# An attention layer with an MLP on one core: one PSUM tile per bank of the running sums, clamp on VectorE, the last batch's mixing moved behind the first pair of output tiles, a second buffer for staged sums

## The chip, the cores and the metric

The kernel runs as one program on one core of a Trainium2 chip. The metric is the device time of an execution in microseconds (us). Three runs of the kernel before took 904.13, 904.23 and 909.96 us; the median is 904.23 us.

## The reference

q, k and v have shape (4, 8, 576, 64): batch, heads, sequence, head width. The MLP works on rows of 512 (all heads side by side), 4 x 576 = 2304 rows, with 2048 hidden columns.

```python
scores = scale * np.matmul(q, k.transpose(0, 1, 3, 2))
x = (np.log1p(np.abs(rel)) / np.log1p(np.maximum(pos[:, None], 1.0)))[..., None]
bias = np.maximum(x @ w1 + b1, 0.0) @ w2
scores = scores + bias.transpose(2, 0, 1)[None]
attn = softmax(scores)                       # over the last axis
x = matmul(attn, v), heads side by side      # (B, S, 512)
u = x + (x.transpose(0, 2, 1) @ U @ V).transpose(0, 2, 1)
out = u + np.maximum(u @ w_ch1, 0.0) @ w_ch2
```

U, V, w_ch1 and w_ch2 arrive as 64-bit floats and are turned into 32-bit floats in the kernel.

## The kernel before

**Attention.** Batch and pair of heads give 16 pairs; each has nine slots of scores, softmax, transposes and products with v. The mixing with U and V (mix_t, mix_h) follows for each batch, and its rows go to u_dram. The code is written out by hand under a manual schedule: the order of the calls is the order on each engine's queue.

**MLP.** The 2304 rows are two sets of 1152 (st = 0, 1), the hidden columns eight blocks of 256 (F). That gives 16 stages n = 8 st + F, counted 0 to 15. In a stage the rows come in two units: u0 with 512 rows (matmuls 256 columns wide) and u1 with 640 rows (320 wide). mlp1 forms a unit's hidden values with seven block products in place of eight. Its four steps are a, b, c and d. Two products are summed on in one PSUM bank after earlier ones (first=False), so a bank is copied out between them:

```python
def a():   # tile p: sums A in bank 0, C in bank 1; tile q: B
    prod(1, k["a"]);  nc.scalar.copy(out=k["r1"], in_=k["a"])
    prod(5, k["c"]);  nc.scalar.copy(out=k["r5"], in_=k["c"])
def b():
    prod(6, k["a"], False);  nc.scalar.copy(out=k["r2"], in_=k["a"])
    prod(3, k["c"], False);  r2 = C + r2      # VectorE, L722
def c():
    prod(7, k["a"], False);  nc.scalar.copy(out=k["r3"], in_=k["a"])
    prod(2, k["b"]);  r3 = r3 + r5;  r1 = B + r1   # L728, L729
def d():
    prod(4, k["a"], False)   # then relu (ScalarE, L735) and the low part (VectorE, L736)
```

Every 32-bit operand is a high and a low part, so a product is six matmuls (L698), named ph in the trace. mlp2 multiplies one tile of 128 hidden rows of the stage before with w_ch2, six matmuls (L761, named po), and VectorE adds the result to acc (L763). A stage runs a, y, b, y, c, y, d, y for u0 with four tiles y, then the same for u1 with five.

**Preparing weights.** Beside the matmuls of stages 1 to 7 the weights of the next stage are converted from 64-bit words (conv): ScalarE size (L1122, L1123), GpSimd clamp (L1126), VectorE shift and join (L1132, L1136), GpSimd add (L1141), and a store to wy_dram. w1_prep then forms four sums (GpSimd, L648 to L651) and splits all seven blocks into high (ScalarE, L667) and low (GpSimd, L671); w2_prep does it for w_ch2 (L679, L682). These calls stand in a list, and background(n) takes groups from its front after each step, spread over the whole stage. Stages 8 to 15 load the converted words again.

**Rows of u.** build_u loads two tiles of u rows, transposes them on TensorE (L587, named tu), copies them (L593, L603), forms four sums (L609 to L612) and splits them (L623, L627). The first set's rows are built late in attention and in stage 0, the second set's in stages 7 and 8.

**Tiles and waits.** PSUM comes from pools: psS has two buffers of two banks, psT one and psT2 two of one bank (used in turn for tag t), psA one. An instruction waits for the engines that last used the same tile. p holds A and C in one tile.

Of the kernel before, what the change touches and what calls it, by code (L numbers as in the profile page):

```python
# [20 lines left out]
DM = H * D  # L21
# [29 lines left out]
PROD = {1: (0, 0), 2: (1, 1), 3: (6, 2), 4: (2, 6), 5: (3, 3), 6: (4, 4), 7: (5, 5)}  # L51
# [5 lines left out]
def kernel(  # L57
# [33 lines left out]
    p1, p2 = ExitStack(), ExitStack()  # L91

    def left(ctx, name, bufs, **kw):
        return ctx.enter_context(tc.tile_pool(name=name, bufs=bufs, side="left", **kw))
# [6 lines left out]
    mix = left(p1, "mix", 1)  # L101
# [26 lines left out]
    ptp = left(p1, "ptp", 1)  # L128
# [278 lines left out]
    def get_pt(p, hf):  # L407
        d = pair[p]
        if ("pt", hf) not in d:
            n, a = (320, LINE) if hf == 0 else (256, 0)  # L410
            t = ptp.tile([P, a + 9 * n], F32, tag=f"pt{hf}", name="pt")[:, a:]
            d["pt", hf] = t.rearrange("p (k q) -> p k q", k=9)
        return d["pt", hf]
# [220 lines left out]
    def w1_op(F, o, low):  # L634
        w = w1q[F]
        return w["b"][o][low] if o < 3 else w["t"][low][:, o - 3]

    def w1_prep(F, ys, t):

        y0, y1 = (y.rearrange("p (k f) -> p k f", k=2) for y in ys)  # L640
        b11, b12 = y0[:, :, 0:P], y0[:, :, P:]
        b21, b22 = y1[:, :, 0:P], y1[:, :, P:]
        tv = ops_view(t)
        both = y1.rearrange("p k (o f) -> p o k f", o=2)

        def sums():
            g = nc.gpsimd
            g.tensor_tensor(out=tv[:, 0], in0=b12, in1=b11, op=ALU.subtract)  # L648
            g.tensor_tensor(out=tv[:, 1], in0=b22, in1=tv[:, 0], op=ALU.subtract)
            g.tensor_tensor(out=tv[:, 2], in0=b22, in1=b12, op=ALU.subtract)  # L650
            g.tensor_tensor(out=tv[:, 3], in0=b21, in1=tv[:, 1], op=ALU.subtract)  # L651

        def trips(which):
            w = w1q[F]
            if "b" in which:
                yield *w["b"][0], b11
                if "two" in w:
                    yield *w["two"], both
                else:
                    yield *w["b"][1], b21  # L660
                    yield *w["b"][2], b22
            if "t" in which:
                yield *w["t"], tv

        def high(which):
            for h, _, x in trips(which):
                nc.scalar.copy(out=h, in_=x)  # L667

        def low(which):
            for h, l, x in trips(which):  # L670
                nc.gpsimd.tensor_tensor(out=l, in0=x, in1=h.bitcast(F32), op=ALU.subtract)  # L671

        return sums, high, low
# [12 lines left out]
    def mlp1(st, F, u, hid, rp):  # L686
# [183 lines left out]
    def open_tail():  # L870
# [5 lines left out]
        tl_p["b22"] = tp.tile([P, LINE + 4 * P], F32R, tag="b", name="w1b")[:, LINE:]  # L876
# [27 lines left out]
    def at_slot(p, s):  # L904
# [8 lines left out]
        elif (p, s) == (NP - 3, 1):  # L913
# [3 lines left out]
            }  # L917
        elif (p, s) == (NP - 3, 8):
# [12 lines left out]
        elif (p, s) == (NP - 2, 6):  # L931
            t = rawp.tile([P, QKW], F32R, tag="raw", name="w1t")
            w1q[0] = {
                "b": [hi_lo(x) for x in (*tl_p["spare"], tl_p["b22"])],
                "t": (ops_view(t[:, 0 : 8 * P]), ops_view(t[:, 8 * P : 16 * P])),
            }
# [7 lines left out]
        elif (p, s) == (NP - 1, 0):  # L944
            tl_p["prep"][1]("bt")
        elif (p, s) == (NP - 1, 1):
            tl_p["prep"][2]("bt")
            tl_p["u1h"] = big_u(2, 1)[0]
        elif p == NP - 1 and 4 <= s <= 8:
            b[0, 1][s - 3]()  # L950
            if s == 6:
                acc_tile(0)
            if s == 8:
                b[1, 0][0]()
# [18 lines left out]
    feed = iter(())  # L973
# [28 lines left out]
    def run(*steps):  # L1002
        for o in steps:
            o()

    hid_t = {}

    def hid(g, u):
        def get():
# [5 lines left out]
            t = hid_t["p"].tile([P, 4 * UNITS[1]], F32R, tag="h", name="hh")  # L1015
            return t[:, 0 : 2 * UNITS[1]], t[:, 2 * UNITS[1] :]
# [10 lines left out]
    run(m[0][0])  # L1027
    slot(NP, 1)
    acc_tile(2)
    run(b[1, 0][1], b[1, 0][2], m[0][1], b[1, 0][3], m[0][2], b[1, 1][0], b[1, 0][4])  # L1030
    slot(NP, 2)
    acc_tile(4)
    run(m[0][3], b[1, 0][5], b[1, 1][1], b[1, 1][2])
    run(y[0], b[1, 1][3], b[1, 2][0])
# [43 lines left out]
    def sum_tile():  # L1078
        return sump.tile([P, 1024], F32, tag="s", name="s")

    def w1_ready(g):
# [3 lines left out]
        def sums():  # L1085
            w1_tile(g)
            k["p"] = w1_prep(g, k["y"], sum_tile())
            k["p"][0]()

        def high():  # L1090
            k["p"][1]("bt")

        def low():
            k["p"][2]("bt")

        return k["y"], [sums, high, low]
# [9 lines left out]
    def conv(src, ys, dst):  # L1106
# [18 lines left out]
        def clamp():  # L1125
            nc.gpsimd.tensor_scalar(  # L1126
# [39 lines left out]
    def conv_groups(n):  # L1166
# [14 lines left out]
        queue.extend(groups)  # L1181

    def w1_y(F, i):
        if F < 2:
            return wq_dram[2 * i : 2 * i + 2, :, F * 2 * P : (F + 1) * 2 * P].rearrange("k p f -> p k f")
        return wy_dram[4 * F + i].rearrange("p (k f) -> p k f", k=2)

    def w2_y(F, j):
        return wq_dram[4 + 2 * F + j] if F < 2 else wy_dram[4 * F + 2 + j]
# [15 lines left out]
    def second_u():  # L1205

        def rows():
# [137 lines left out]
```

## Time and profile before

| | us |
|---|---|
| median of three runs | 904.23 |
| the profiled execution | 905.67 |
| its span, first to last instruction | 903.9 |
| PE busy / DVE / ACT / POOL | 766.7 / 511.3 / 445.6 / 419.7 |

The span is what the trace covers; 1.8 us of the profiled execution lie around it. PE is TensorE's matmuls, DVE VectorE, ACT ScalarE, POOL GpSimd. A matmul's busy time runs into that of the next one, since they are pipelined; so the time of a group is read from start to start. A row by stretch gives its bounds and length, the busy time of PE, PEld (weight load), DVE, ACT and POOL with the number of instructions, the granted clock, the DMA share and GB/s. A wait's three numbers are the total, how often, and the longest. In a timeline the bracket at the end of a row gives how long the engine sat idle before it, and who ended that.

### The profile page before, as it was taken

The numbers are of one execution on the slowest core, as the hardware profiler recorded it, in microseconds if no ns is written. First come the engines' busy times: TensorE is split into PE (matmuls) and PEld (weight loads), VectorE is DVE, ScalarE is ACT, GpSimd is POOL, SyncE is SP. The second block draws the span as 40 slices with busy tenths as digits, with TensorE's granted clock in tenths as the row PEclk, the third lists the DMA queues.
The fourth block names the chain that finished last, engine by engine and source line by source line (L and its number), as shares of the span: only waits on it lengthen the run. The fifth ranks groups of instructions, "written<-read, shape, count | busy, mean of one in ns | idle before, by whom it ended". The sixth has DMA issues, their size and how long they took to land. (4 is left out here: it accounts for less than half of the span.)

```text
span 903.9 us, 13221 instructions
## 1 busy us (share of the span) xinstructions
PE 766.7 (85%) x4748; PEld 609.0 (67%) x4748; DVE 511.3 (57%) x1085; ACT 445.6 (49%) x982; POOL 419.7 (46%) x321
## 2 busy tenths in 40 slices
PE   6788999999999978868877877878546999989998
PEld 3346777877776766657766766766435878878876
DVE  7965778777687665533655455444433344434434
ACT  7976677776767667423433433424322323233320
POOL 0025457655664473226777677656521433244310
PEclk9999999999999999996999899899677999999999
DMA  6989954556545531252222332332233311011002
GB/s 192 300 288 270 257 134 131 140 142 167 153 106 133 155 101 48 82 181 70 70 84 91 106 91 83 106 94 63 74 109 111 111 36 44 26 48 48 24 1 106
DMA packets 49218, 103.37 MB, mean 114 GB/s; under 512 B 7808, under 2 KB 12416, under 8 KB 47104
## 3 DMA queue, kind: packets, MB, share of 16 engines
q1 hardware_dynamic: 48912, 102.26, 38.4%
q8 instruction: 38, 0.62, 0.3%
q10 hardware_dynamic: 240, 0.26, 0.1%
q14 instruction: 28, 0.23, 0.1%
HBM read 73.78 MB, written 28.72 MB: 113 GB/s over the span
## 5 line engine op out<-in xcount | busy, mean ns | idle before, releaser
L698 PE MATMUL ph<-u,w 128*128 128x256 f32 (+1 forms) x1260 | 216.6, 313 | 73.1 <-ACT r L714 36.6
L698 PEld LDWEIGHTS ph<-u,w 128*128 128x128 f32 x1260 | 192.1, 200 | 103.5 <-ACT r L714 44.0
L763 DVE TENSOR_TENSOR acc<-po,acc 128x512 f32<-128x512 f32 x144 | 98.8, 689 | 156.1 <-PE po L761 154.4
L761 PE MATMUL po<-u,hh 128*128 128x512 f32 x648 | 180.1, 407 | 3.3 <-DVE acc L763 3.0
L761 PEld LDWEIGHTS po<-u,hh 128*128 128x128 f32 x648 | 118.8, 195 | 24.7 <-DVE acc L763 4.3
L376 ACT ACTIVATE p<-p,st 128x576 f32<-128x576 f32 x128 | 99.9, 781 | 43.9 <-DVE st L357 43.9
L357 DVE CUSTOM_DVE_ANT_0 p<-sc,bias 128x576 f32<-128x576 f32 x128 | 96.0, 750 | 39.9 <-PE sc L355 31.3
L355 PE MATMUL sc<-hi 128*128 128x288 f32 x320 | 101.4, 333 | 2.8 <-DVE st L357 2.7
L355 PE MATMUL sc<-lo,hi 128*128 128x288 f32 x320 | 90.1, 297 | 5.0 <-POOL lo L178 5.0
L461 PE MATMUL o<-pt,v 128*64 128x320 f32 (+1 forms) x640 | 91.2, 412 | 2.7 <-ACT pt L403 2.7
L172 POOL TENSOR_SCALAR hi<-raw 128x1216 fp32r<-128x1216 f32 x30 | 36.4, 1212 | 101.6 <-DMA raw<-in_qk_dram 85.1
L425 PE MATMUL tb<-ident,p 128*128 128x128 f32 x512 | 77.5, 274 | 2.8 <-DVE x_sb L405 2.3
L355 PEld LDWEIGHTS sc<-hi 128*128 128x128 f32 x320 | 60.7, 190 | 20.1 <-issue 10.7
L461 PEld LDWEIGHTS o<-pt,v 128*64 128x64 f32 x640 | 45.1, 136 | 37.9 <-ACT pt L403 7.3
L403 ACT COPY pt<-tb 128x512 f32<-128x512 f32 x88 | 50.9, 579 | 29.1 <-PE tb L425 28.2
L355 PEld LDWEIGHTS sc<-lo,hi 128*128 128x128 f32 x320 | 60.9, 190 | 6.5 <-POOL lo L178 5.9
L425 PEld LDWEIGHTS tb<-ident,p 128*128 128x128 f32 x512 | 61.8, 141 | 5.0 <-ACT p L376 4.1
L761 PE MATMUL po<-w,hh 128*128 128x512 f32 x216 | 64.2, 407 | 0.0
L671 POOL TENSOR_TENSOR w<-y,w 128x256 fp32r<-128x256 f32 (+1 forms) x30 | 29.8, 1015 | 61.4 <-ACT w L667 61.4
L1141 POOL TENSOR_TENSOR y<-wt,y 128x512 int32<-128x512 int32 x24 | 37.5, 1564 | 44.5 <-ACT wt L1122 14.1
L1126 POOL TENSOR_SCALAR wt<-wt 128x512 f32<-128x512 f32 x24 | 45.9, 1914 | 21.5 <-ACT wt L1122 21.5
L627 POOL TENSOR_TENSOR u<-sb,u 128x1024 fp32r<-128x1024 f32 (+1 forms) x10 | 22.4, 2244 | 63.9 <-ACT u L623 52.7
(129 smaller groups left out, 1241.5 us busy)
## 6 DMA issues: line engine op xcount, KB each, us to landing
raw<-in_qk_dram SPq DMA_DIRECT2D x31, 608.0 KB, 7.3
wraw<-in_w_ch_dram SPq DMA_DIRECT2D x24, 512.0 KB, 3.9
bias_dram<-ring SPq DMA_DIRECT2D x26, 295.5 KB, 4.2
wy_dram<-y SPq DMA_DIRECT2D x24, 256.0 KB, 2.2
y<-wy_dram SPq DMA_DIRECT2D x24, 256.0 KB, 2.6
v<-in_vp_dram SPq DMA_DIRECT2D x16, 320.0 KB, 8.2
bias<-bias_dram SPq DMA_DIRECT2D x16, 288.0 KB, 4.7
acc<-u_dram SPq DMA_DIRECT2D x18, 256.0 KB, 3.0
```

The lines of the kernel that those rows point to most:

```text
L172: nc.gpsimd.tensor_scalar(out=hi[:, a:e], in0=raw[:, a:e], scalar1=1.0, scalar2=0.0, op0=ALU.mult, op1=ALU.add)
L355: mm(ps[:, a, 0:HALF], lhsT=hi[:, q0 : q0 + P], rhs=kk, start=(i == 0), stop=(i == n - 1))
L357: nc.vector.tensor_tensor_reduce(out=halves(dst), in0=ps[:, :, 0:HALF], in1=halves(bias[hp][:, s * S : (s + 1) * S]), scale=-0.125, scalar ...
L376: nc.scalar.activation(out=dst, in_=dst, func=AF.Exp, bias=st[:, s : s + 1], scale=-1.0, accum_out=st[:, 10 + s : 11 + s])
L403: nc.scalar.copy(out=out, in_=in_)
L425: nc.tensor.transpose(bank[:, kb, :], src[:, b0 + kb * P : b0 + (kb + 1) * P], ident)
L461: mm(o[hd * D : (hd + 1) * D, 0:n], lhsT=v[:, vb * D : (vb + 1) * D], rhs=pt[:, pb, :], start=(j == 0), stop=(j == 4),)
L698: mm(out, lhsT=w1_op(g, w, a)[:, kt], rhs=b[:, o, kt, :], start=(first and c == 0), stop=(c == 5), skip_group_check=not first,)
L761: mm(ps, lhsT=lhs(x, f), rhs=w, start=(c == 0), stop=(c == 5))
L763: nc.vector.tensor_tensor(out=acc[i], in0=ps, in1=acc[i], op=ALU.add)
L1126: nc.gpsimd.tensor_scalar(out=k["t"].bitcast(F32), in0=k["t"].bitcast(F32), scalar1=F64_LO, scalar2=F64_HI, op0=ALU.max, op1=ALU.min,)
L1141: nc.gpsimd.tensor_tensor(out=k["y"], in0=k["t"], in1=k["y"], op=ALU.add)
```

## The change

It gives A and C a tile of psS each, and B a one-bank tile of tag t when its product comes. The clamp of conv goes to VectorE. w1_prep writes one of its sums over its input and splits the seven blocks in three groups of 512, 512 and 768 columns, each with its own steps. The rows of stage 0 are built earlier, with a staging buffer of their own for one of them (st); the weights of stage 1 are prepared in stage 0 in memory of their own. mix_t of the last batch stands behind the fourth output tile, and mix_h in stage 1. The work beside the matmuls is set by a plan, which spreads a list of groups over given steps. In stages 7 and 8 the rows of u use the buffers of conv.

```diff
         def a():
-            k["p"], k["q"] = psum("s", [P, 2, 512], "ph"), psum("s", [P, 2, 512], "ph")
-            k["a"], k["c"], k["b"] = k["p"][:, 0, 0:n], k["p"][:, 1, 0:n], k["q"][:, 0, 0:n]
+            k["a"], k["c"] = (psum("s", [P, 2, 512], "ph")[:, 0, 0:n] for _ in range(2))
...
         def c():
             prod(7, k["a"], False)
             nc.scalar.copy(out=k["r3"], in_=k["a"])
+            k["b"] = psum("t", [P, 512], "ph")[:, 0:n]
             prod(2, k["b"])
...
         def clamp():
-            nc.gpsimd.tensor_scalar(
+            nc.vector.tensor_scalar(
                 out=k["t"].bitcast(F32), in0=k["t"].bitcast(F32),
                 scalar1=F64_LO, scalar2=F64_HI, op0=ALU.max, op1=ALU.min,
             )
...
-                    then = ((1, 4, 5) if i else (), (1, 2))[g == n]
+                    then = ((1, 1, 2, 4, 5, 5, 6) if i else (), (2, 3))[g == n]
...
+            b[1, 1] = build_u(0, 1, 1, tl_p["row"], lambda k: tl_p["st"][:, (k == "sb") * 1024 :])
...
-    run(m[0][0])
+    run(b[1, 0][4], m[0][0], b[1, 0][5])
...
+    ts = [pmp.tile([P, S], F32, tag="praw", name="wt")[:, 0 : 4 * P], tl_p["row"]()[:, 0 : 2 * P]]
+    prep = w1_prep(1, ys, ts, True)
+    run(y[0], b[1, 2][4], b[1, 2][5], prep[0])
     slot(NP, 4)
-    run(b[1, 1][4], y[1], b[1, 1][5])
+    run(y[1], m[1][0])
     slot(NP, 8)
-    run(y[2], b[1, 2][1])
+    prep[1](1)
+    run(y[2], m[1][1])
...
     mix_t(B - 1)
-    run(b[1, 2][3], b[1, 2][4], b[1, 2][5], y[3])
-    mix_h(B - 1, 4)
-    run(m[1][0])
...
-    o = again(1, 0)
-    run(o[0], o[1], late_y[0], o[2], o[3], late_y[1], late_y[2])
...
         if n == 1:
-            first, second = [], late_y[3:]
+            h = [lambda c=c: mix_h(B - 1, c) for c in (4, 0, 1, 2, 3)]
+            y0, y1 = y1[0:3], y1[3:]
+            steps = []
+            for i in range(4):
+                steps += m[0][i : i + 1] + y0[i : i + 1] + h[i : i + 1]
...
+        def spread(groups, a, e):
+            for i, g in enumerate(groups):
+                plan[a + i * (e - a) // len(groups)] += g
...
+        else:
+            spread(work, 0, last - 1)
```

TensorE, start of a unit u1 in a late stage (ph_7758 is the tile that holds A and C, w1 the weights, u1_4028 and u1_4206 high and low weights kept beside the rows). Before:

```order
L698 MATMUL ph_7758<-u1_4028,w1_7519 128x320 [waits DVE_49]
L698 MATMUL ph_7758<-u1_4206,w1_7519 128x320
L698 MATMUL ph_7758<-u1_4028,w1_7519 128x320 x2
L698 MATMUL ph_7758<-u1_4206,w1_7519 128x320
L698 MATMUL ph_7758<-u1_4028,w1_7519 128x320
L698 MATMUL ph_7758<-u1_4028,w1_7519 128x320 [waits Activation_49]
```

The sixth row is the first matmul of product 5; it waits for ScalarE's copy of product 1 out of the same tile. The same place now (ph_7777 holds A, ph_7778 C):

```order
L699 MATMUL ph_7777<-u1_4026,w1_7504 128x320 [waits DVE_49]
L699 MATMUL ph_7777<-u1_4226,w1_7504 128x320
L699 MATMUL ph_7777<-u1_4026,w1_7504 128x320 x2
L699 MATMUL ph_7777<-u1_4226,w1_7504 128x320
L699 MATMUL ph_7777<-u1_4026,w1_7504 128x320
L699 MATMUL ph_7778<-u1_4026,w1_7504 128x320 [waits DVE_49]
```

Product 5 has the tile that held A in the unit before, and waits for VectorE's last read of it there (L737, L736 in the kernel before).

ScalarE, from the end of one stage into the next, among stages 3 to 6 (w is the high part of w_ch2; r and hh are mlp1's). Before:

```order
L726 COPY r<-ph 128x320 [waits DVE_49,PE_49]
L735 ACTIVATE hh<-r 128x960 [waits DVE_49]
L735 ACTIVATE hh<-ph 128x320 [waits PE_49]
L679 CAST w_4541<-y 128x512 [waits Pool_49]
L714 COPY r<-ph 128x256 [waits PE_49,Activation_49]
```

The cast waits for GpSimd's add of the last conversion, and the copy of product 1 stands behind it. In the changed kernel a cast that waits for GpSimd stands there too, and one more in the middle of the stage, between u0's relu and u1's copy:

```order
L736 ACTIVATE hh<-r 128x768 [waits DVE_49]
L736 ACTIVATE hh<-ph 128x256 [waits PE_49]
L666 CAST w_5118<-y 128x512 [waits Pool_49]
L1145 ACTIVATE wt<-wraw 128x512 [waits DMAHW6_49]
L1146 ACTIVATE y<-wraw 128x512 [waits DMAHW1_49,Activation_49]
L714 COPY r<-ph 128x320 [waits PE_49,Activation_49]
```

The casts of the split blocks have come forward, from behind u1's copies to ahead of them.

VectorE, a conversion at the turn from u0 to u1 of such a stage (wt and wraw are conv's). Before:

```order
L1132 TENSOR_SCALAR wt<-wt 128x512 [waits Pool_49]
L1136 SCALAR_TENSOR_TENSOR wt<-wraw,sgn,wt 128x512 [waits DMAHW4_49,DVE_49]
L736 SCALAR_TENSOR_TENSOR hh<-r,hh 128x768 [waits Activation_49]
L736 SCALAR_TENSOR_TENSOR hh<-ph,hh 128x256 [waits Activation_49]
L763 TENSOR_TENSOR acc<-po,acc 128x512 [waits PE_49] x2
```

And now:

```order
L1149 TENSOR_SCALAR wt<-wt 128x512 [waits Pool_49]
L764 TENSOR_TENSOR acc<-po,acc 128x512 [waits PE_49]
L1155 TENSOR_SCALAR wt<-wt 128x512 [waits DVE_49]
L1159 SCALAR_TENSOR_TENSOR wt<-wraw,sgn,wt 128x512 [waits DMAHW4_49,DVE_49]
L737 SCALAR_TENSOR_TENSOR hh<-r,hh 128x768 [waits Activation_49]
```

The clamp (L1149) has joined the queue a step ahead of the shift, and an acc addition stands between them.

## Rows read from the trace of the kernel before

**Rows 1.** The page: TensorE's granted clock, in 40 slices of the span.

```profile
PEclk9999999999999999996999899899677999999999
```

**Rows 2.** Busy time by stretch: stage 0, 1, 2, 3-6, 7, 8, 9-15.

```profile
357.29:402.43 45.14, 35.82 (x206) 26.48 (x204) 22.23 (x44) 17.83 (x35) 9.38 (x5) 1.00 0.31 101
402.43:431.63 29.20, 21.41 (x97) 18.34 (x97) 8.84 (x14) 11.29 (x22) 21.02 (x19) 0.71 0.30 102
431.63:460.47 28.84, 25.35 (x138) 21.17 (x139) 16.02 (x23) 13.74 (x26) 22.09 (x17) 1.00 0.26 82
460.47:595.90 135.43, 107.28 (x553) 90.77 (x552) 70.00 (x108) 52.39 (x100) 95.78 (x69) 0.92 0.28 94
595.90:640.29 44.39, 29.19 (x156) 23.80 (x154) 22.55 (x34) 16.05 (x29) 22.43 (x17) 0.91 0.29 89
640.29:699.40 59.11, 37.98 (x160) 31.25 (x161) 19.62 (x38) 16.96 (x29) 18.40 (x14) 0.75 0.26 86
699.40:887.00 187.60, 172.91 (x968) 149.83 (x967) 81.17 (x134) 59.36 (x117) 65.30 (x56) 1.00 0.14 42
```

**Rows 3.** Waits of TensorE, whole span: total us, times, longest.

```profile
PE ph L698 <- ACT r L714: 38.8, 32, 5.3
PE tu L587 <- DMA y<-u_dram: 17.6, 6, 5.7
PE ph L698 <- ACT r L720: 16.7, 32, 1.5
```

**Rows 4.** The chain that ended last, in stage 15: start, us, what.

```profile
860.25 0.72 PE ph L698 x6
861.47 0.97 PE ph L698 x6
...
872.29 0.89 PE ph L698 x6
873.74 1.15 PE ph L698 x6
...
884.23 15.33 PE po L761 x66
```

**Rows 5.** Timeline, from stage 3 into stage 4.

```profile
492.67 1.91 POOL L1126 TENSOR_SCALAR wt<-wt 128x512 f32<-128x512 f32 x1
...
495.96 2.05 POOL L1141 TENSOR_TENSOR y<-wt,y 128x512 int32<-128x512 int32 x1 [1.39 <-issue]
...
498.04 0.62 ACT L679 CAST w<-y 128x512 fp32r<-128x512 f32 x1 [4.75 <-POOL y L1141]
...
498.99 1.65 PE L698 MATMUL ph<-u,w 128*128 128x256 f32 x6 [5.31 <-ACT r L714]
```

**Rows 6.** Timeline: a GpSimd split and a VectorE sum at one time.

```profile
488.79 2.39 POOL L671 TENSOR_TENSOR w<-s,w 128x1024 fp32r<-128x1024 f32 x1
...
488.99 2.53 DVE L728 TENSOR_TENSOR r<-r,r 128x320 f32<-128x320 f32 x1 [2.54 <-ACT r L726]
```

**Rows 7.** VectorE's shift in the first conversions (a line's own view, 60 to 240).

```profile
L216 DVE TENSOR_SCALAR wt<-wt x15: 229/295/2876, 105.7 to 237.4; 128x256 int32<-128x256 int32 x13, 128x160 int32<-128x160 int32 x1, 128x128 int32<-128x128 int32 x1
```

**Rows 8.** TensorE's timeline ahead of stage 1.

```profile
402.43 0.50 PE L698 MATMUL ph<-u,w 128*128 128x256 f32 x2 [3.42 <-ACT w L667]
405.90 1.22 PE L698 MATMUL ph<-u,w 128*128 128x256 f32 x4 [2.97 <-POOL w L671]
```

**Rows 9.** TensorE's timeline: a flip in stage 7, and one in stage 8.

```profile
629.58 0.66 PE L587 MATMUL tu<-ident,y 128*128 128x128 f32 x4
629.99 1.65 PE L761 MATMUL po<-u,hh 128*128 128x512 f32 x6
...
671.95 1.09 PE L587 MATMUL tu<-ident,y 128*128 128x128 f32 x4 [5.71 <-DMA y<-u_dram]
```

**Rows 10.** Groups by line: the clamp, and VectorE's shift of the same width.

```profile
L1126 POOL TENSOR_SCALAR wt<-wt 128x512 f32<-128x512 f32 x24 | 45.9, 1914 | 21.5 <-ACT wt L1122 21.5
...
L1132 DVE TENSOR_SCALAR wt<-wt 128x512 int32<-128x512 int32 x24 | 10.1, 423 | 24.7 <-POOL wt L1126 24.7
```

More of the change, by code (lines that the diff above doesn't have):

```diff
@@ L100 @@
     vpp = left(ctx, "vpp", 2)
-    mix = left(p1, "mix", 1)
+    ptp = left(ctx, "ptp", 1)
+    mix = left(p3, "mix", 1, "right")
     bias_dram = dram.tile([S * H + 8, PITCH], F32, name="bias_dram")
@@ L634, in w1_op @@
     def w1_op(F, o, low):
[L635 to L644, printed above, removed]
+        g, i = ((0, 0), (0, 1), (1, 0), (1, 1), (2, 0), (2, 1), (2, 2))[o]
+        return w1q[F][g][low][:, i]
@@ L651, in sums @@
[L651 to L666, printed above, removed]
-                nc.scalar.copy(out=h, in_=x)
@@ L673, in w1_prep, with high, low @@
+        def high(g):
+            for h, _, x in trips(g):
+                nc.scalar.copy(out=h, in_=x)
+        def low(g):
+            for h, l, x in trips(g):
+                (nc.vector if fast and g < 2 else nc.gpsimd).tensor_tensor(
+                    out=l, in0=x, in1=h.bitcast(F32), op=ALU.subtract
+                )
         return sums, high, low
@@ L971, in pool, with w1_y, w2_y, run @@
         return left(ctx, name, bufs, reuse_waits="tile")
-    feed = iter(())
+    def w1_y(F, i):
+        if F < 2:
+            return wq_dram[2 * i : 2 * i + 2, :, F * 2 * P : (F + 1) * 2 * P].rearrange("k p f -> p k f")
+        return wy_dram[4 * F + i].rearrange("p (k f) -> p k f", k=2)
+    def w2_y(F, j):
+        return wq_dram[4 + 2 * F + j] if F < 2 else wy_dram[4 * F + 2 + j]
+    def run(*steps):
+        for o in steps:
+            o()
     for p in range(NP):
@@ L1085, in sums, with group, rest @@
         def sums():
-            w1_tile(g)
-            k["p"] = w1_prep(g, k["y"], sum_tile())
-            k["p"][0]()
[L1090 to L1096, printed above, removed]
+            if g % 2:
+                w1q[g] = w1q[1]
+            else:
+                t = hid_t["w1"].tile([P, W1 + LINE], F32R, tag="w1", name="w1")
+                w1q[g] = [hi_lo(t[:, a * P : e * P]) for a, e in ((0, 8), (8, 16), (16, 28))]
+            k["p"] = w1_prep(g, k["y"], [sum_tile()])
+            k["p"][0]()
+        def group(g):
+            k["p"][1](g)
+        def rest(g):
+            k["p"][2](g)
+        return k["y"], [sums] + [lambda o=o, g=g: o(g) for g in (1, 0, 2) for o in (group, rest)]
     def w2_ready(g):
@@ L1180, in conv_groups @@
             groups.pop()
[L1181 to L1189, printed above, removed]
+        return groups
     def again(g, which):
@@ L1232 @@
                 o = again(g, which)
[L1233 to L1252 removed]
+                ahead.append(o[0])
+                work += [[]] * 2 * (which == 0) + [[x] for x in o[1:]]
+        if n == 1:
+            spread(work[0:8], 0, cut - 1)
+            spread(work[8:], cut, last)
+        elif n == NF - 1:
+            spread(work, 0, 9)
+            uop[1, 0], uop[1, 1] = uop[0, 0], uop[0, 1]
+            spread([[o] for j in range(2) for o in again_u[0, j]] + [again_u[1, 0][0:1]], 8, last)
+        elif n == NF:
+            spread([[o] for j in range(3) for o in again_u[1, j][j == 0 :]], 0, cut)
+            spread(work, 0, last - 1)
+        else:
+            spread(work, 0, last - 1)
+        if n != 1:
+            run(*ahead)
         loaded = 0
@@ L1255 @@
             o()
+            if n == 1 and i == cut - 1:
+                run(*ahead)
+            run(*plan[i])
             if n == NF and i >= 8:
```

198 lines of the change are left out of this document (98 added, 100 removed).

## Prediction

> **What bounds the kernel now.** I read the stretches first, with the granted clock, then the waits of TensorE, the chain, and timelines of the places where TensorE waits.
>
> Until the last pair of attention the two kernels issue the same work in the same order, so the sum starts with the end of stage 0 [rows 2]. From there on PE does the most work in every stretch but stage 1: 172.91 of 187.60 us in stages 9 to 15, 107.28 of 135.43 in stages 3 to 6. So the bound is PE plus what it waits for. In stages 9 to 15 the clock is 1.00 (the 2.4 GHz level) all along; it falls to 0.71 to 0.92 in the stretches with long waits, and the page shows the dips there too [rows 1].
>
> The waits are of three kinds [rows 3]. One is for ScalarE's copy of A (L714, 38.8 us) ahead of product 5, and one for the copy ahead of product 3 (L720, 16.7 us). Product 5 writes C, and product 3 adds to C: neither needs the copy that it waits for, only a bank in the same tile. I call these false waits. The third is for rows of u on their way from memory (17.6 us).
>
> What a stage takes with nothing to wait for comes from the chain in stage 15 [rows 4]: a product is 0.72 us at 256 columns and 0.89 at 320, an output tile (six matmuls) 15.33 / 11 = 1.39. So 7 x 0.72 + 7 x 0.89 + 9 x 1.39 = 23.8 us. Stages 9 to 15 took 187.6 / 7 = 26.8 each, 3.0 more. The chain shows where: 861.47 follows the end 860.97 of the product before by 0.50, and the restarted product lasts 0.97 in place of 0.72, together 0.75. In the wide unit it is 0.56 and 0.26, together 0.82. Two such waits a unit, four a stage, make 3.1. So stages 9 to 15 are the product of unit prices plus the false waits, and hold nothing else.
>
> **The change, part by part.** All sums go against the profiled execution (span 903.9, own time 905.67, that is span + 1.8); the median of the runs is 1.4 below it.
>
> *A tile for each bank.* The false waits go. In stages 9 to 15 that is 187.6 - 7 x 23.8 = 21.0 us. Nothing else is late there: product 6 does add to A and still waits for the copy L714, but product 5 and the output tile lie between, over 2 us, where the wait for it was 0.50. Least: 14, if a third came back as new waits (below). Most: 21.
>
> *The new wait.* Product 5 now takes the tile that held A in the unit before, whose last reader is VectorE's L737 (L736 before). Behind it stand all matmuls of the unit. In late stages that reader has an output tile and product 1, 1.39 + 0.72 at least, of cover, and VectorE is busy 81.17 of 187.60 us [rows 2]. I take 0 there and about 0.3 a stage in stages 2 to 7, where conversions stand in VectorE's queue.
>
> *Stages 3 to 6.* They take 135.43, or 33.9 each, 10.1 above 23.8. Besides the 3.1 of false waits, one false wait a stage is long: the copy of A stands on ScalarE behind a cast of w_ch2 that waits for GpSimd's add, and that add stands behind a clamp of 1.91 and itself takes 2.05; ScalarE sat 4.75 us and PE 5.31 [rows 5]. The clock, 0.92, takes some 8% of about 27 busy us, 2 a stage. Without product 5's false wait PE has product 5 and an output tile, 2.3 us, before product 6 asks for the copy, and the clamp of 1.91 is gone from the GpSimd queue. I leave 1.35 for product 6 in mid-stage, where a cast of the split blocks now stands ahead of u1's copy, and 1.05 for contention and the new wait: 26.2 a stage, 104.8 in all, -30.6. Bounds: 23.8 a stage if all is covered (-40.2), and 30.8 if only the false waits of 3.1 go (-12.4).
>
> *The clamp.* 24 instructions of 1.914 us leave GpSimd. On VectorE the shift of the same width takes 0.423 [rows 10], so 24 x 0.42 = 10 us come to an engine that is busy 70.00 of 135.43 in stages 3 to 6: no cost on the path by itself, since PE is the busier by 37. Bounds of one clamp: 0.42, and 2.9 by the longest shift of the same form, 2876 ns beside a median of 295 [rows 7], which ran while GpSimd did a split. A VectorE sum of the unit took 2.53 us while GpSimd's split of 2.39 ran [rows 6]. I take 0.42 for most and let the 1.05 of the stage hold the rest, since [rows 10] is the mean of 24 shifts in the same stages.
>
> The Trainium skill says why such a row can be (SBUF — State Buffer, Who interferes with whom): GpSimd and VectorE share a port pair, held for a whole instruction by whichever is first, a VectorE instruction of two inputs needs part of it, and a tensor_scalar can need all of it. The 2.53 us beside the 2.39 agree. By that rule the change moves onto VectorE just the kind of instruction that can be blocked; rival B works it out from rows.
>
> *Start of the MLP.* Stage 0 ends at 402.43. In the new order three output tiles (3 x 1.39 = 4.2) and the 15 matmuls of mix_h (about 3.5, estimated at an output tile's 0.23 a matmul) move into stage 1; the wait of 3.42 for the weights [rows 8] goes, since they are made earlier; and some 3.9 of false waits (five of the 0.78) go. Together -14.9, end at 387.5. The two moved pieces, 7.7, are only shifted, and come back in stage 1: 14 products 11.3 + five output tiles 7.0 + mix 3.5 = 21.8, and 2.2 for weights that must wait until the rows stored by the mixing have left their memory. That is 24.0 against 29.2, where the second piece of the wait for the weights (2.97 [rows 8]) stood and the clock was 0.71: -5.2. Bounds of the two together: -23, all of PE's idle time (74.3 less 57.2 busy is 17.1) and the 6.2 that a clock of 0.71 costs of 21.41; and -7 if the weights are late again by both waits of [rows 8], 6.4, with the same loss of clock.
>
> *Stage 2.* 28.84 to 27.0, -1.8: weights late by 2 and 1.2 in mid-stage. Bounds 23.8 and 28.8.
>
> *Stages 7 and 8.* These hold the second set's rows. A flip is 0.41 from start to start at [rows 9] 629.58. Stage 7: 23.8 + 4 x 0.4 + 1.35 in mid-stage + 1.75 for loads = 28.5 against 44.4, -15.9. In stage 8 PE waited three times for rows of u and once for their split, the longest 5.71 [rows 9], with the clock at 0.75. Now rows are asked for earlier, and u0 is split before stage 8. 23.8 + 5 flips 2.0 + 4.3 for the chain from the last loads to the first product of u1 + 5.1 for loads that stand in the queue behind stores of outputs (two buffers for the rows in place of four) + 1.9 clock and small = 37.1; I take 39, since the loads of the next weights share that queue: -20.1. Bounds for the two: 52 and 90 us.
>
> *End.* From 887.0 the last output tiles and stores, 16.9, are the same.
>
> Sum: -14.9 - 5.2 - 1.8 - 30.6 - 15.9 - 20.1 - 21.0 = -109.5. The span becomes 794.4, the profiled execution 796.2, and against the median 1.4 less: **795 us**.
>
> **The rivals.**
>
> *A. Only the false waits go* (chance 0.15). What stops PE in stages 2 to 8 is then late weights and late rows, which the change leaves late elsewhere. For it: the 4.75 of ScalarE [rows 5] is a real wait that the split of tiles only delays, and two buffers for rows are fewer than four. Stages 2 to 8 took 28.84 + 135.43 + 44.39 + 59.11 = 267.8; less 7 x 3.1 = 21.7 that is 246.1, where the forecast has 199.3. So 795 + 46.8 = 842. Against it: the 5.31 begins at product 5, which no longer asks.
>
> *B. VectorE's clamp is blocked by GpSimd* (0.15). If each clamp waits for half a GpSimd instruction of 2.56 (between 2.39 and 2.876 [rows 6, 7]), 1.28, and that reaches the path each time, 24 x 1.28 = 31: 826. Against it: mean 423 of the shift, whose neighbours are the same.
>
> *C. Slower: the new wait decides* (0.03). Product 5 of each unit waits for VectorE's last subtraction of the unit before, which moves back by clamps, shifts and blocked sums. 30 units have such a wait; at 4 us each, 795 + 120 = 915. The time is over 904 from 3.7 us a unit. For that VectorE must be the later engine all through, also in stages 9 to 15, where it converts nothing.
>
> *D. The change doesn't do what it says* (0.05): a tile of two banks of which one is used may still make products wait for another copy, as both stay in one pool that turns. Then 14 x 3.1 = 43 of false waits stay, and 795 + 43 = 838.
>
> **How the numbers follow.** The forecast has 0.62, A 0.15, B 0.15, D 0.05, C 0.03. All but C are faster by more than 1%, which is about what a measurement of this kernel can tell from no change; between A and no change lie 60 us, for which I leave 0.02 out of the forecast's and A's tails: faster 0.95, same 0.02, slower 0.03. Low end: my allowances for stalls in stages 1 to 8 (2.2, 3.2, 4 x 2.4, 3.1, 13.2) are 31; with 19 of them gone the time is 776. The high end takes in B, D and A: 844.
>
> **What would show it.** Right: in the waits of TensorE the copy L714 is far below 38.8 and stands only at product 6; the copy L720 is gone; stages 9 to 15 last 23.8 each at clock 1.00; the clamps on VectorE last about 0.42; product 5 waits for VectorE less than 5 us in all. Wrong for A: stages 3 to 6 over 30 us each with the copy L714 or the weights as releaser. For B: a mean clamp over 1 us, and VectorE ahead of PE in the chain. For C: L737 as the first releaser of PE. The single number that decides most is the length of stages 3 to 6, then that of stage 8.

## The result, and the profile after

The changed kernel takes 807.94 us in the median (four executions), the kernel before 904.51 beside it: a ratio of 0.8915 (95% interval 0.8878 to 0.8951), 10.8% faster. A second set of four gave 805.65 and a ratio of 0.8877 (0.8831 to 0.8923). The forecast was 795 with a range of 776 to 844. One of the first four executions, the profiled one, was disturbed as a whole (1784 us), so the rows below are of the profiled execution of the second set: its own time is 805.16, its span 803.4.

Its busy time by stretch, stages 0, 1, 2, 3, 4, 5, 6, 7, 8 and 9 to 15; the columns are those of [rows 2]:

```profile
359.24:386.09 26.85, 25.11 (x165) 19.78 (x163) 14.27 (x30) 14.59 (x30) 11.44 (x9) 1.00 0.33 102
386.09:410.43 24.34, 22.03 (x131) 19.50 (x130) 14.88 (x27) 10.44 (x22) 9.01 (x9) 1.00 0.52 175
410.43:439.35 28.92, 24.80 (x140) 20.93 (x139) 21.55 (x30) 14.03 (x27) 20.55 (x16) 1.00 0.27 89
439.35:464.00 24.65, 24.18 (x139) 21.17 (x138) 19.95 (x31) 11.26 (x23) 16.48 (x13) 1.00 0.38 120
464.00:492.55 28.55, 24.53 (x139) 21.04 (x138) 22.30 (x33) 14.64 (x28) 18.06 (x15) 1.00 0.37 118
492.55:518.74 26.19, 25.71 (x140) 22.60 (x139) 20.05 (x31) 11.27 (x23) 16.48 (x13) 0.93 0.34 113
518.74:547.33 28.59, 24.57 (x139) 21.04 (x138) 23.07 (x34) 14.59 (x28) 18.10 (x15) 1.00 0.35 119
547.33:580.01 32.68, 28.87 (x155) 25.64 (x154) 23.67 (x37) 15.58 (x29) 16.81 (x13) 0.90 0.40 126
580.01:620.95 40.94, 29.81 (x160) 25.23 (x159) 23.34 (x36) 16.50 (x29) 20.76 (x13) 0.92 0.33 117
620.95:786.50 165.55, 164.88 (x967) 148.06 (x966) 81.59 (x135) 59.53 (x117) 66.07 (x56) 1.00 0.16 48
```

Look first at the last row: PE is busy 164.88 of 165.55 us, where [rows 2] has 172.91 of 187.60. Hardly a wait is left to take away there. Then at the lengths of stages 2 to 6: 28.9, 24.7, 28.6, 26.2, 28.6. Each even stage is about 4 us longer than stage 3, at the same clock of 1.00. The waits of TensorE over the whole span say why (total, times, longest); of the attention's waits one row is shown:

```profile
PE bs L284 <- ACT ring L272: 8.7, 5, 6.0
PE tu L587 <- DMA row<-u_dram: 8.4, 3, 4.8
PE ph L699 <- DVE hh L737: 8.3, 6, 1.7
PE po L762 <- DVE acc L764: 5.4, 3, 1.8
...
PE tu L587 <- DVE r L730: 2.6, 1, 2.6
...
PE ph L699 <- ACT r L714: 1.8, 5, 0.4
...
PE ph L699 <- ACT r L720: 0.9, 1, 0.9
```

The copies L714 and L720, 38.8 and 16.7 us in [rows 3], are down to 1.8 and 0.9, and TensorE waits for L714 five times in place of 32. In their place stands VectorE: product 5 waits for L737, the reader of A one unit back (the wait that the change adds), and an output tile waits for L764, which frees its bank. All of the output tiles' waits for L764 and 5.1 of the 8.3 us for L737 fall in stages 2, 4 and 6. TensorE's timeline at the start and the end of stage 4:

```profile
464.00 0.85 PE L699 MATMUL ph<-u,w 128*128 128x256 f32 x6
466.55 0.96 PE L699 MATMUL ph<-u,w 128*128 128x256 f32 x6 [1.69 <-DVE hh L737]
...
491.06 0.73 PE L762 MATMUL po<-u,w1c 128*128 128x512 f32 x2 [1.81 <-DVE acc L764]
```

1.69 + 1.81 = 3.5 of the 4 us. Stage 5 has no wait for VectorE, and is still 1.5 us longer than stage 3: right behind the 1.81 the granted clock is down (0.93 over the stage, 1.00 in stage 3), and its first two products take 1.45 and 1.48 us, where those of stage 3 take 0.87. What VectorE and GpSimd did ahead of the second wait (VectorE first):

```profile
485.35 0.92 DVE L1155 TENSOR_SCALAR wt<-wt 128x512 int32<-128x512 int32 x1
486.30 2.22 DVE L1159 SCALAR_TENSOR_TENSOR wt<-wraw,sgn,wt 128x512 int32<-128x512 int32 x1
488.44 1.56 DVE L729 TENSOR_TENSOR r<-r,r 128x320 f32<-128x320 f32 x1
489.93 0.48 DVE L730 TENSOR_TENSOR r<-ph,r 128x320 f32<-128x320 f32 x1
490.33 0.68 DVE L764 TENSOR_TENSOR acc<-po,acc 128x512 f32<-128x512 f32 x1
```

```profile
484.50 1.48 POOL L670 TENSOR_TENSOR w1c<-y,w1c 128x512 fp32r<-128x512 f32 x1
485.94 2.03 POOL L670 TENSOR_TENSOR w1b<-s,w1b 128x768 fp32r<-128x768 f32 x1
487.93 1.73 POOL L683 TENSOR_TENSOR u<-y,u 128x512 fp32r<-128x512 f32 x1
```

VectorE never waits in these rows; its instructions are long. The join L1159 takes 2.22 (median of all 24: 0.753), the sum L729 takes 1.56 (median of its 32, both widths: 0.492), the shift 0.92 in place of 0.42: together about 3 us, by which the last acc addition comes later. Each long one lies over a GpSimd split. This is the behaviour of [rows 6], now on the path.

The first wait of stage 4 has the same cause, one stage end earlier. VectorE, then GpSimd, at the end of stage 3:

```profile
459.75 2.21 DVE L1159 SCALAR_TENSOR_TENSOR wt<-wraw,sgn,wt 128x512 int32<-128x512 int32 x1
461.88 1.58 DVE L729 TENSOR_TENSOR r<-r,r 128x320 f32<-128x320 f32 x1
```

```profile
459.39 2.02 POOL L670 TENSOR_TENSOR w<-s,w 128x768 fp32r<-128x768 f32 x1
461.37 1.74 POOL L683 TENSOR_TENSOR u<-y,u 128x512 fp32r<-128x512 f32 x1
```

So VectorE is late at the end of each of the stages 2 to 6, even and odd. After an even stage TensorE pays for it at the last output tile, after an odd one at product 5 of the next stage; both payments fall within an even stage. The wait at the start of stage 2 is another matter: the sum ahead of it took 0.49 us.

### The profile page after: what moved, and what is told of

Its sections match the earlier page's. It is cut to its first block, busy times and chain, and to the rows that moved or that the text cites. A ratio compares the mean times of both kernels' runs of the same rounds, so it can differ in the third digit from the quotient of the medians.

```text
span 1782.3 us, 13217 instructions
## 1 busy us (share of the span) xinstructions
PE 1769.5 (99%) x4748; PEld 1227.2 (69%) x4748; DVE 553.7 (31%) x1113; ACT 456.7 (26%) x982; POOL 361.7 (20%) x293
## 4 chain that ended last, share of the span: by engine, by line
PE 99%; DVE 0%; DMA 0%; ACT 0%; SPq 0%; issue 0%; DVEq 0%
PE po L762 29%; PE ph L699 25%; PE sc L355 12%; PE o L461 12%; PE tb L425 9%; PE bs L284 4%; PE tu L587 1%; PE ti L442 1%; PE mt L500 1%; PE tm L433 1%; PE tx L479 1%; PE mh L520 1%; PE mh L521 1%; PE mh L519 1%; PE ti L445 0%; PE tx L481 0%
## 5 line engine op out<-in xcount | busy, mean ns | idle before, releaser
L762 PE MATMUL po<-u,hh 128*128 128x512 f32 x568 | 370.6, 830 | 0.0
L762 PEld LDWEIGHTS po<-u,hh 128*128 128x128 f32 x568 | 200.9, 369 | 88.8 <-issue 85.8
L764 DVE TENSOR_TENSOR acc<-po,acc 128x512 f32<-128x512 f32 x144 | 99.6, 692 | 482.0 <-PE po L762 481.9
L461 PE MATMUL o<-pt,v 128*64 128x320 f32 (+1 forms) x640 | 218.7, 898 | 0.0
L355 PE MATMUL sc<-hi 128*128 128x288 f32 x320 | 202.4, 632 | 0.0
L425 PE MATMUL tb<-ident,p 128*128 128x128 f32 x512 | 183.1, 538 | 0.0
L355 PE MATMUL sc<-lo,hi 128*128 128x288 f32 x320 | 182.2, 570 | 0.0
L699 PE MATMUL ph<-u,w1b 128*128 128x256 f32 (+1 forms) x480 | 175.9, 567 | 0.0
L699 PEld LDWEIGHTS ph<-u,w1b 128*128 128x128 f32 x480 | 160.7, 387 | 20.1 <-issue 14.5
L284 PE MATMUL bs<-ring,small_sb 128*32 128x512 f32 (+17 forms) x352 | 74.9, 1064 | 6.0 <-ACT ring L272 6.0
L699 PEld LDWEIGHTS ph<-u,w1c 128*128 128x128 f32 x192 | 64.7, 364 | 17.0 <-issue 15.3
L1164 POOL TENSOR_TENSOR y<-wt,y 128x512 int32<-128x512 int32 x24 | 33.5, 1396 | 207.6 <-DVE wt L1159 124.5
```

The lines of the kernel that those rows point to most:

```text
L284: mm(bs[T][32 * cg : 32 * cg + 32, a // 512, 0 : min(n - a, 512)], lhsT=w2_sb, rhs=hids[T][cg][:, a : min(n, a + 512)], start=True, stop=True,
L355: mm(ps[:, a, 0:HALF], lhsT=hi[:, q0 : q0 + P], rhs=kk, start=(i == 0), stop=(i == n - 1))
L425: nc.tensor.transpose(bank[:, kb, :], src[:, b0 + kb * P : b0 + (kb + 1) * P], ident)
L461: mm(o[hd * D : (hd + 1) * D, 0:n], lhsT=v[:, vb * D : (vb + 1) * D], rhs=pt[:, pb, :], start=(j == 0), stop=(j == 4),)
L699: mm(out, lhsT=w1_op(g, w, a)[:, kt], rhs=b[:, o, kt, :], start=(first and c == 0), stop=(c == 5), skip_group_check=not first,)
L762: mm(ps, lhsT=lhs(x, f), rhs=w, start=(c == 0), stop=(c == 5))
```

## The experiments

All times are medians; each ratio is to the kernel before, run beside it on the same chip.

**The changed kernel again.** No edit.

> The changed kernel, unchanged, for a profile at the ordinary pace. Theory (the sum of the prediction): 808 us as in the runs, 13 over the 795 forecast; stages 9 to 15 last 23.8 each, and the 13 stand in stages 1 to 8, most of them in stages 3 to 6 or 8. Rival (stages 9 to 15 keep a wait of their own, on VectorE or on ScalarE): 25 to 25.6 each, which alone makes 9 to 13 us.

Measured: 805.65. Stages 9 to 15 hold 165.55 / 7 = 23.65 each, so the rival is out: all that the forecast missed lies in stages 2 to 8, as the rows above show.

**A and C in one tile again.**

```diff
-            k["a"], k["c"] = (psum("s", [P, 2, 512], "ph")[:, 0, 0:n] for _ in range(2))
+            k["p"], k["q"] = psum("s", [P, 2, 512], "ph"), psum("s", [P, 2, 512], "ph")
+            k["a"], k["c"], k["b"] = k["p"][:, 0, 0:n], k["p"][:, 1, 0:n], k["q"][:, 0, 0:n]
...
-            k["b"] = psum("t", [P, 512], "ph")[:, 0:n]
```

> The changed kernel with A and C in one tile of two banks again, B in a second tile of the same pool. Theory (false waits are the largest part): stages 9 to 15 go back to 26.8 each (+21), and stages 1 to 8 gain 0.75 to 0.8 at each of four places a stage and more where ScalarE stands behind GpSimd: +25 to +45; in all 854 to 874 us. Rival (the plan of the work and the clamp do most): +10 to +25, 818 to 833 us.

Measured: 855.59, ratio 0.9419 (0.9379 to 0.9459), as the theory said. (B goes back into the pool of A and C with it.) The waits came back whole:

```profile
PE ph L699 <- ACT r L715: 33.8, 32, 3.0
PE ph L699 <- ACT r L721: 19.7, 32, 2.9
```

The false waits are worth 50 us in the changed kernel, half of its gain. Stages 10 to 15 last 26.6 to 26.7, about as before the change (26.8). Stages 3 to 6 are 30.6 to 30.7 each: the even ones lose less by the joined tile than the odd ones, which fits VectorE's lateness hiding in part behind the false waits.

**The clamp on GpSimd again.**

```diff
-            nc.vector.tensor_scalar(
+            nc.gpsimd.tensor_scalar(
```

> The changed kernel with the clamp on GpSimd as before. Theory: GpSimd gains 24 x 1.91 = 46 us in stages 1 to 7, VectorE loses 10; the casts that wait for GpSimd's add come up to 1.9 later, one or two of them a stage on the path: +1 to +2 a stage, 815 to 822 us. Rival (shared port: the clamp on VectorE is blocked and blocks others): no slower than the changed kernel, 795 to 808 us. Rival (idle GpSimd hides it): 808 us within 1%.

Measured: 841.38, ratio 0.9257 (0.9215 to 0.9298): 36 us slower than the changed kernel, so all three expectations fall. Not GpSimd's 46 us of work costs this, but where VectorE stands meanwhile. The two engines late in stage 4 (VectorE, then GpSimd), and TensorE's waits in that stage:

```profile
502.84 0.68 DVE L764 TENSOR_TENSOR acc<-po,acc 128x512 f32<-128x512 f32 x1
508.30 1.48 DVE L1155 TENSOR_SCALAR wt<-wt 128x512 int32<-128x512 int32 x1 [4.78 <-POOL wt L1149]
509.81 0.75 DVE L1159 SCALAR_TENSOR_TENSOR wt<-wraw,sgn,wt 128x512 int32<-128x512 int32 x1
510.48 0.48 DVE L729 TENSOR_TENSOR r<-r,r 128x320 f32<-128x320 f32 x1
```

```profile
503.29 1.29 POOL L670 TENSOR_TENSOR w1c<-y,w1c 128x512 fp32r<-128x512 f32 x1
504.53 1.85 POOL L670 TENSOR_TENSOR w1b<-s,w1b 128x768 fp32r<-128x768 f32 x1
506.35 1.92 POOL L1149 TENSOR_SCALAR wt<-wt 128x512 f32<-128x512 f32 x1
```

```profile
PE po L762 <- DVE acc L764: 5.9, 2, 5.1
PE ph L699 <- DVE hh L737: 5.0, 1, 5.0
```

The clamp stands on GpSimd behind two splits, the shift stands at the head of VectorE's queue and waits for the clamp, and the sum L729 of the unit stands behind the shift with nothing to wait for but its turn. Over the kernel the shift waits 65.0 us so; in the kernel before it was 24.7 [rows 10]. Stages 2, 4 and 6 take 34.9, 40.4 and 39.2, while the odd 3 and 5 take 26.4 and 27.0.

**The kernel before with parts of the change.** Three kernels: the tiles alone, the clamp alone (each by the line of the change), and both.

> The kernel before with only the tiles for A, C and B changed (one tile a bank, B in a one-bank tile). Theory: -21 in stages 9 to 15, -3.1 in each of stages 1 to 8 and part of the 4 to 5 us waits of stages 3 to 6, for which product 6 asks 2.3 us later: 904 - 21 - 25 - 8 = 850 us. Rival (only false waits of the common size go): 904 - 45 = 859 us. Rival (the tiles do nothing without the rest): 904 us.

> The kernel before with only the clamp on VectorE. Theory: the cast of w_ch2 and the copy behind it come about 1.5 us earlier in stages 2 to 7, so 904 - 9 = 895 us. Rival (port: the clamp costs VectorE as much as it saves): 904 us within 1%. Rival (GpSimd's queue held up VectorE everywhere, as the run with the clamp on GpSimd suggests): 870 to 880 us.

> The kernel before with the tiles for each bank and the clamp on VectorE, all else as before. Theory (the two add up): 868 less what the clamp alone gives, 855 to 860 us, so that the new plan, start and rows of u are worth some 50. Rival (with the false waits gone the clamp is on the path, as in the changed kernel where it was worth 35): 833 us.

Measured:

| kernel | us | ratio (interval) |
|---|---|---|
| tiles alone | 868.35 | 0.9567 (0.9522 to 0.9613) |
| clamp alone | 890.17 | 0.9809 (0.9756 to 0.9861) |
| both | 849.38 | 0.9370 (0.9336 to 0.9404) |

The tiles alone gave less than both forecasts of a gain (850 and 859), and both together came out between theory (855 to 860) and rival (833). The tiles alone give 4.3%, less than the 50 us of the joined tile would say: stages 9 to 15 are down to 23.7, but in the stages of conversion VectorE takes the place of the copy. TensorE's waits with the tiles alone:

```profile
PE ph L698 <- DVE hh L736: 21.3, 8, 4.6
```

(The edits are those lines of the diff of the change.) The clamp alone gives 1.9% (1.4 to 2.4), twice what was expected. Both give 6.3%, the sum of the two (4.3 + 1.9). So the new plan, the earlier start and the rows of u are worth the rest, 0.9370 - 0.8877 = 4.9%. In the profiled runs of this kernel with both and of the changed one that is 17 us up to the end of stage 0 (403.1 against 386.1), 4.6 in stage 2 (33.5 against 28.9), 3.7 in stage 7 and 16.4 in stage 8 (57.3 against 40.9); stage 1 is the same within 0.6, and stages 3 to 6 together differ by 4.5 only.

**GpSimd fills zeros in place of the low splits.** The low parts of the weights of w_ch1 that are made from stage 1 on are left out. They are three a stage, 42 in all; the count of 18 in the expectation is wrong.

```diff
-                (nc.vector if fast and g < 2 else nc.gpsimd).tensor_tensor(
-                    out=l, in0=x, in1=h.bitcast(F32), op=ALU.subtract
-                )
+                if fast:
...
+                else:
+                    nc.gpsimd.memset(l.bitcast(F32), 0.0)
```

> The changed kernel in which GpSimd's 18 splits of w_ch1's blocks a pair of stages (L670) only fill the low parts with zeros from stage 1 on: GpSimd writes there and reads nothing; the low parts are left out of the result, the matmuls are the same. Theory (VectorE is late because its two-input instructions and GpSimd's splits hold each other up): the join at the end of stages 2, 4 and 6 goes from 2.22 us to 0.75 and the sum behind it from 1.57 to 0.6; the waits of 1.7 (product 5 for VectorE) and 1.8 (output tile for acc) go to under 0.5 each, stages 2, 4 and 6 from 28.7 to 25.5, about 10 us in all: 796 us. Rival (VectorE is late because of what stands in its queue, whatever GpSimd does): the waits stay over 1 us each, 803 to 808 us.

The second kernel:

```diff
+                    for _ in range(3):
+                        nc.gpsimd.memset(l.bitcast(F32), 0.0)
```

> As the run with zero fills, but each fill is written three times, 3 x 0.53 to 0.63 = 1.6 to 1.9 us, about as long as the split that it stands for (1.30 to 2.03); the low parts are again left out of the result. It tells apart two readings of the 11 us that the zero fills gave. Theory (the reads of GpSimd's splits stretch VectorE's instructions): the join at the end of stages 2, 4 and 6 stays near 0.75 and the time is 796 to 799 us. Rival (GpSimd's shorter queue made the rest earlier): 803 to 808 us.

Measured: 795.76, ratio 0.8796 (0.8755 to 0.8838), with one fill, as the theory said, and 801.58, ratio 0.8833 (0.8795 to 0.8871), with three, which lies between the theory's 796 to 799 and the rival's 803 to 808; so the trace has to decide there. Stages 2 to 6 are 127.1 and 131.4 us in the profiled executions, against 136.9. With one fill stages 4 and 6 go from 28.6 to 24.7 and 24.5, while stage 2 stays at 28.8 (one wait of 2.4 for VectorE, at its start). The place of the two timelines above, with three fills (VectorE, then GpSimd):

```profile
487.63 0.81 DVE L1159 TENSOR_SCALAR wt<-wt 128x512 int32<-128x512 int32 x1
488.48 0.75 DVE L1163 SCALAR_TENSOR_TENSOR wt<-wraw,sgn,wt 128x512 int32<-128x512 int32 x1
489.15 0.48 DVE L733 TENSOR_TENSOR r<-r,r 128x320 f32<-128x320 f32 x1
```

```profile
486.31 1.86 POOL L676 MEMSET w1c<- 128x512 f32 x3
488.11 2.62 POOL L676 MEMSET w1b<- 128x768 f32 x3
490.69 1.29 POOL L687 TENSOR_TENSOR u<-y,u 128x512 fp32r<-128x512 f32 x1
```

GpSimd works all through the join and the sum, for longer than its split took (2.62 against 2.03), and both of these VectorE instructions have their short time: it is not that GpSimd is busy, but what it does. The shift ahead of them stays long (0.81) beside the fills, so this holds for the two with two inputs, 2.5 of the 3 us. Stages 4 and 6 lost 2.4 and 2.5 us, and stages 3 to 6 are level at 26.1 to 26.2 (stage 3 gained 1.5 in length). So the stretch of join and sum is shown to come from the split. By the Trainium skill (SBUF — State Buffer, Who interferes with whom) a VectorE instruction with two inputs in SBUF is in the way of a GpSimd instruction that reads there, and not of one that only writes; this pair of runs agrees, 2.22 against 0.75 us.

That three fills are still 6 us over one fill fits GpSimd's longer queue: TensorE waited 4.3 us in all for GpSimd's split of w_ch2 (L687, five times). The intervals of the two overlap, and that of three fills overlaps the changed kernel's too, so the division of the 10 us (some 4 to 6 for the stretch, the rest for the queue) rests on the stage lengths of one profiled execution each, and that the queue has the rest is argued.

**The same work one step later,** in stages 2 to 6.

```diff
+        elif n < NF - 1:
+            spread(work, 1, last)
         else:
             spread(work, 0, last - 1)
```

> The changed kernel with the plan of the work of stages 2 to 6 spread over the steps 1 to the last in place of 0 to the last but one: all conversions come about one step later. Theory (the wait comes from the place of one conversion ahead of u1's sums): shift and join fall behind the sums of the unit, the relu is earlier, stages 2, 4 and 6 lose about 2 us each: 800 us. Rival (the weights are just in time): the first products of the next stage wait for the split of their weights, 2 or more a stage: 815 to 820 us.

Measured: 806.93, ratio 0.8914 (0.8878 to 0.8950, which overlaps the intervals of both runs of the changed kernel): no difference, where the theory had 800 and the rival 815 to 820. Stages 2 to 6 are 29.6, 25.7, 29.1, 25.6, 29.1. Join and splits moved together, so the one still lies over the other: the last join of a stage takes 1.66 beside the split of w_ch2, the sums of both units 0.83. In stages 2 to 6 TensorE's waits for VectorE fell by a tenth only (9.4 us in place of 10.5), and those for the copy L714 rose from 1.8 to 8.6.

**Low splits on VectorE.** First the longest of the three alone, then all three, from stage 1 on.

> The changed kernel with the longest of the three low splits of a stage (768 columns, 1.85 to 2.03 on GpSimd) on VectorE, from stage 1 on. Theory: it is the one that lies over the join of 2.22 us; VectorE gets about 1.0 more a stage (0.69 at 512 columns, by width), the join loses up to 1.5 and GpSimd 2: stages 2, 4, 6 lose 1 to 2 each, 801 to 804 us. Rival (the next GpSimd split only comes forward and lies over the join in its place): VectorE has 1.0 more on its queue, 808 to 812 us.

> The changed kernel with all three low splits of w_ch1 of a stage on VectorE. Theory: VectorE gets 0.68 + 0.68 + 1.0 = 2.4 us a stage and loses up to 3.0 of stretch in each stage; GpSimd is freed of 4.5 to 5.5; the splits wait on VectorE's queue for ScalarE's casts, which may hold up the sums behind them: 797 to 806 us. Rival (VectorE's queue is the bound, and a wait at its head holds up every sum behind it): 812 to 820 us.

Measured: 804.06, ratio 0.8845 (0.8810 to 0.8881), and 803.94, ratio 0.8860 (0.8828 to 0.8891). The second lies in its theory's range and the first at the edge of it, but neither can be told from the changed kernel. By stage there is a gain and a loss: with all three, stages 3 to 7 take 132.0 against 140.7, but stage 2 takes 31.8 against 28.9 and stage 8 takes 44.3 against 40.9. In stages 3 to 6 the last join has its 0.75 again and the sum behind it 0.48, a second sign, with the low parts kept, that the split made them long.

**A version from these.** Low splits on VectorE only where they gained, in stages 3 to 7; and in stage 8 the last load of rows one store of outputs earlier on SP's queue.

```diff
-                (nc.vector if fast and g < 2 else nc.gpsimd).tensor_tensor(
+                (nc.vector if (fast and g < 2) or 4 <= F <= NF else nc.gpsimd).tensor_tensor(
...
-            spread([[o] for j in range(3) for o in again_u[1, j][j == 0 :]], 0, cut)
+            u0, u1, u2 = (again_u[1, j] for j in range(3))
+            spread([[o] for o in u0[1:] + u1[0:3] + u2[0:1] + u1[3:] + u2[1:]], 0, cut)
```

> A version from the runs: the low splits of the weights for stages 4 to 8 (made in stages 3 to 7) on VectorE, those for stage 3 and from stage 9 on stay on GpSimd; and in stage 8 the last load of rows of u is issued one store of outputs earlier on SP's queue. Theory: stages 3 to 7 as in the run with all low splits on VectorE, 132 in place of 141, stage 2 stays 29, stage 8 loses the wait of 4.8 us for that load: 806 - 9 - 4 = 793 us. Rival for stages 3 to 7 (their gain comes back in stage 8, where the runs with low splits on VectorE were 2 to 3 longer): 798 us. Rival for the load (the wait is for the row buffer and not for the store): stage 8 keeps a wait over 3 us for rows.

Measured: 800.35, ratio 0.8807 (0.8779 to 0.8836); its slowest execution (800.96) is below the fastest of the changed kernel (805.15), though on another chip. Some 0.7% faster than the changed kernel, with intervals that touch, but slower than both expectations (793 and 798). Stages 2 to 7 came as expected (28.9, then 131.9 in all). Stage 8 did not: 44.2. TensorE's waits in stage 8, of the changed kernel and then of this one:

```profile
PE tu L587 <- DMA row<-u_dram: 6.1, 2, 4.8
PE ph L699 <- DVE u L627: 2.6, 2, 1.6
...
```

```profile
PE ph L699 <- DVE u L627: 6.6, 2, 4.3
PE ph L699 <- ACT u L623: 2.7, 1, 2.7
PE tu L587 <- DMA row<-u_dram: 1.4, 1, 1.4
...
```

The wait for rows went from 6.1 to 1.4, so the load did stand behind a store. SyncE's queue in the changed kernel (the stores, then the last loads) shows it:

```profile
593.91 5.62 SPq L767 DMA_DIRECT2D out_dram<-acc  x2
599.63 1.09 SPq L582 DMA_DIRECT2D row<-u_dram  x2
```

But the first products of u1 then waited for the rows' split, and run on 31.9 us into the stage in place of 30.6. Behind that long wait the granted clock was 0.50 (the 1.2 GHz level) for 3.1 us, and the eleven matmuls there took 3.30 us; in the changed kernel they took 1.89 at a clock of 1.00. From them to the end of the stage it is 12.3 us against 10.3. On VectorE, ahead of the split, a subtraction of 0.95 us (L737) took 2.53 while GpSimd's split of the rows (2.41) ran, but it took 2.63 in the changed kernel too and is not the difference. The earlier load bought nothing here. Nor is stage 8 shown to be longer by the low splits on VectorE: it took 44.3 with all three there, but 43.8 with the single zero fills, where VectorE has none of them (41.9 with three fills). Why it grows when the stages ahead of it shrink stays open.

## Why the prediction was right, and where it was off

Against the profiled execution, its own steps:

| term | forecast | measured |
|---|---|---|
| end of stage 0 | 387.5 | 386.1 |
| stage 1 | 24.0 | 24.3 |
| stage 2 | 27.0 | 28.9 |
| stages 3 to 6 | 104.8 | 108.0 |
| stage 7 | 28.5 | 32.7 |
| stage 8 | 39.0 | 40.9 |
| stages 9 to 15 | 166.6 | 165.6 |
| end | 16.9 | 16.9 |
| span | 794.4 | 803.4 |

*Right: the floor and the false waits.* The floor of 23.8 us a stage, from unit prices of the chain, is what stages 9 to 15 now take (23.65), and putting the joined tile back cost 50 us at the places named. Rival D is out: TensorE waits 1.8 and 0.9 us in all for the two copies, and stages 9 to 15 are at the floor.

*Right: the start, and stage 8 in size.* Up to the end of stage 1 the sum is off by 1.1 us. That the moved pieces account for it, and not something else in the new order, was not tried apart. In stage 1 it is luck in part: the 2.2 was left for late weights, and TensorE waited there 1.4 for L737 and 0.9 for L720 instead.

*Off: the term of the new wait.* "About 0.3 a stage in stages 2 to 7" was among the smallest terms of the sum (in stages 3 to 6 a part of the 1.05 for contention and the new wait) and carried most of the error. L737 cost 1.7 at product 5 in stages 2, 4 and 6 and 1.2 in stage 7, and an output tile waited 1.8 more for acc in each of stages 2, 4 and 6, which the sum didn't have at all: some 10 us over the term, where the span is 9.0 over the forecast. The mechanism is that of rival C, at under a tenth of its price: 8.3 us for L737 over the kernel, 0.7 of it in stages 9 to 15. What failed in the step is that VectorE's busy share (half of the stretch) was taken for its lateness: it needs only one stretched join in the wrong place, just ahead of a unit's sums. The clock that stage 5 loses behind such a wait, 1.5 us, isn't in the sum either.

*Off the other way: product 6.* I left 1.35 a stage for its wait for the copy L714; it took 0.4. By luck this hid part of the error above.

*Rival B was half right.* Its clamp of 1.70 (0.42 + 1.28) is there in four of 24 only: these take 1.34 to 1.37 beside a GpSimd add and split, the median is 0.429, the mean 0.60. But the blocked pair of engines cost more elsewhere: on the two-input instructions, join and sum, beside the split. I priced it for the moved instruction, and it fell on its neighbours, which [rows 6] had shown on just such a sum.

*Too small: what the clamp gives.* The step took the clamp only as time on GpSimd and 10 us on VectorE. In the changed kernel it is worth 36 us, because VectorE's queue no longer stops behind GpSimd's. The sum came out right since stages 3 to 6 were built up from the floor, and not from the gains of the edits.

*Stage 7*, 4.2 over: a flip waited 2.6 us for a bank that VectorE's L730 still had to read (B now takes a bank of the flips' tag), and the clock was 0.90. Both are missing in the step; which of them is worth how much wasn't tried.

Rival A (stages 2 to 8 at 246 in place of 199) came to 210.5: a quarter of the way.

## What to carry to other kernels

Two results in one tile make the second one's writer wait for the first one's reader; where a matmul waits 0.5 us for a copy of something that it doesn't touch, give each bank its tile, and look next at who reads the bank that it gets instead. Work beside the critical engine is judged by where it stands in a queue, not by its sum: a step that waits for another engine at the head of a queue holds up everything behind it, here 36 us for 24 small instructions. A gain counted up from the floor of a stage with few allowances is safer than one counted down from the waits seen, since each wait removed uncovers the next.

## What the runs showed of the hardware

A VectorE instruction with two SBUF operands that ran into a GpSimd split took three to five times as long: 0.75 to 2.22 us for the join, 0.49 to 1.56 and up to 2.63 for the sum, 0.95 to 2.53 for the subtraction. In the rows of stage 4 above, join and sum end 0.55 and 0.34 us after the split that ran when they began. Which engine began first decides in these two and in the reverse case: a subtraction that began 0.23 us ahead of GpSimd's add kept its 0.95 us, and the add (L1164) took 1.87 in place of 1.29, in the changed kernel's stage 4. GpSimd's own splits grew less than VectorE's instructions, 1.30 to 1.75 us at 512 columns.

Zero fills by GpSimd left join and sum at their short times, though they ran beside them as long as the split had. They did not leave the clamp and the shift so, which have one input: in the run with three fills the shift beside them took 0.81 in each of stages 2 to 6 in place of 0.42, and the clamp beside them (and the end of a GpSimd add) 0.99 to 1.75 in place of 0.43.
